# A one-column GELU on ScalarE behind its DMA issues, so that one table set serves an early copy and the GELUs

## The chip, the core and the metric

The kernel runs on one core of a Trainium2 chip. The metric is the device time of one execution, in microseconds (us). A kernel is run several times; medians and ranges are given. Engines are named as the profile names them: PE (matmul), PEld (PE's weight loads), ACT (ScalarE), DVE (VectorE), POOL (GpSimd), SP (its queue issues most DMAs). PSUM is the memory that PE writes its results to. A table load (`ACT_TABLE_LOAD` in the traces) is an instruction that the compiler puts on ACT; in before there is one ahead of the first copy, one ahead of the first GELU and one ahead of the first exp. A "slab" of a weight is 128 of its rows.

## The reference, cut to what matters

Two mixers read the same `x` (2048 x 512) and their results are blended with a gate. The change touches only the start of the second mixer, B:

```python
def _B_ref(x, w_in, w_sp, b_sp, w_out):
    Fh = w_in.shape[-1] // 2                      # 688
    z = gelu_tanh(x @ w_in)
    z1, z2 = z[..., :Fh], layernorm(z[..., Fh:])
    g = w_sp @ z2 + b_sp                          # over the sequence
    return (z1 * g) @ w_out
# mixer A: softmax feature maps (exp), linear attention; later in the kernel
# out = g * A(x) + (1 - g) * B(x)
```

## The kernel before: the parts that matter

The kernel first computes `z2` and `z1` tile by tile (128 rows each): PE multiplies, and ACT applies GELU to the result in PSUM and writes it to `z2all` or `z1all`. Later come the exps of mixer A. At the start, rows 0 to 255 of `x` arrive by plain DMA in `xs` and are transposed on PE; three of the four transposed pieces are copied to `xT` by DVE, and one by ACT:

```python
nc.sync.dma_start(out=xs[:, 0, :], in_=x2[0:P, :])
nc.scalar.dma_start(out=w_z2[:, 0, 0:HF], in_=w_in_v[:, 0, FH:FH + HF])
nc.sync.dma_start(out=xs[:, 1, :], in_=x2[P:2 * P, :])
load_z2w(nc.scalar, 1)            # w_z2 slabs 1..3 on ACT's DMA queue
load_z2w(nc.scalar, 2)
nc.sync.dma_start(out=w_z2[:, 0, HF:FH], in_=w_in_v[:, 0, FH + HF:F])
load_z2w(nc.scalar, 3)
x_dma_T(2, 2)                     # rows 256..511 of x, transposing DMA
for h in range(2):                # w_z1
    nc.sync.dma_start(out=w_z1[:, 2 * h:2 * h + 2, :], in_=...)
for i in range(4, 8):
    x_dma_T(i)
# ...
def zp_tile():                    # three PSUM tiles in turn
    return psA.tile([P, 2, CH], FP32, name="zp", tag=next_turn("zp", 3))

def z2_out(tt, zp):
    nc.scalar.activation(out=z2v, in_=zp[:, :, 0:HF], func=AF.Gelu_apprx_tanh)
    nc.vector.tensor_copy(out=glog[:, tt:tt + 1], in_=zp[:, 1, HF:HF + 1])
    # ... bn_stats, bn_aggr on DVE

def z2_first_two():               # tiles 0 and 1; order of PE's work
    warm_up(6); warm_up(2, P)     # matmuls on constants
    x_T(0, 0, 1, ...); x_T(0, 1, NDT, ...)
    warm_up(3, P)
    one(0, 0, 0)                  # one(tile, slab of w_z2, half)
    x_T(1, 0, 2, ...)
    x_T(1, 2, NDT, ..., on_act=True)     # <- the one copy on ACT
    one(0, 1, 0); warm_up(1, P); one(1, 0, 0); one(1, 1, 0)
    gate_T()
    one(0, 2, 0); one(1, 2, 0)
    for dt in range(1, 3):
        one(0, dt, 1); one(1, dt, 1)
    for tt in range(2):
        one(tt, 3, 0); one(tt, 0, 1); one(tt, 3, 1)
        z2_out(tt, zps[tt])       # <- the first GELU
# then z2_tile(2), z2_tile(3), z1 tiles 0..3, z2 tiles 4..7, ...
# b_T() (a small matmul on "brow") stands behind z1 tile 7

def x_T(i, d0, d1, tp, on_act=False):
    # ... PE transposes into tp
    if on_act:
        nc.scalar.copy(out=dst, in_=tp)
    else:
        nc.vector.tensor_copy(out=dst, in_=tp)
```

The softmax here doesn't subtract the row's maximum and nothing guards it: scores larger than these inputs give would overflow.

Of the kernel before, what the change touches and what calls it, by code (L numbers as in the profile page):

```python
# [7 lines left out]
AF = mybir.ActivationFunctionType  # L8
# [3 lines left out]
BF16 = mybir.dt.bfloat16  # L12
I32 = mybir.dt.int32

P = 128
# [20 lines left out]
def kernel(  # L36
# [14 lines left out]
    nc = tc.nc  # L51
# [6 lines left out]
    early = early_cm.__enter__()  # L58
# [45 lines left out]
        out=ramp[:, 0, :], data0=ones32[:, :], data1=zeros[:, :], initial=0.0,  # L104
# [4 lines left out]
    for q in range(4):  # L109
        qs = slice(32 * q, 32 * q + 32)  # L110
        nc.vector.tensor_tensor(
            out=ident[qs, qs], in0=ramp[qs, 0, :], in1=ramp[qs, 1, :], op=ALU.is_equal)
# [3 lines left out]
    def load_z2w(eng, dt):  # L116
        eng.dma_start(out=w_z2[:, dt, 0:FH], in_=w_in_v[:, dt, FH:F])  # L117
# [5 lines left out]
    load_z2w(nc.scalar, 2)  # L123
    nc.sync.dma_start(out=w_z2[:, 0, HF:FH], in_=w_in_v[:, 0, FH + HF:F])
    load_z2w(nc.scalar, 3)

    def x_dma_T(i, n=1):
        nc.sync.dma_start_transpose(out=xT[:, :, i * P:(i + n) * P], in_=x2[i * P:(i + n) * P, :])

    x_dma_T(2, 2)  # L130
    for h in range(2):
        nc.sync.dma_start(
            out=w_z1[:, 2 * h:2 * h + 2, :], in_=w_in_v[:, 2 * h:2 * h + 2, 0:FH])
    for i in range(4, 8):
        x_dma_T(i)
    for q in range(2, NCH):
        nc.sync.dma_start_transpose(
            out=xT[:, :, q * CH:(q + 1) * CH], in_=x2[q * CH:(q + 1) * CH, :]
        )
    nc.sync.dma_start(out=brow[0:NT, :], in_=B_b_sp.rearrange("(t p) -> t p", p=P))  # L140
    for qk in (1, 0):
        nc.sync.dma_start_transpose(
            out=wqkT[:, qk * NDT:(qk + 1) * NDT, :], in_=A_wqkv[:, qk * D:(qk + 1) * D])
# [4 lines left out]
    for h in range(2):  # L148
        nc.sync.dma_start(
            out=wv_sb[:, 2 * h:2 * h + 2, :],  # L150
            in_=A_wqkv[h * 2 * P:(h + 1) * 2 * P, 2 * D:3 * D].rearrange("(dt p) n -> p dt n", p=P),
        )
    for q in range(NCH):
        nc.sync.dma_start_transpose(
            out=wspT[:, :, q * CH:(q + 1) * CH], in_=B_w_sp[q * CH:(q + 1) * CH, :]
# [4 lines left out]
        out=mask4[:], in_=mask4[:], pattern=[[-32, NG]],  # L160
# [3 lines left out]
        out=mask4[:], in_=mask4[:], pattern=[[32, NG]],  # L164
# [3 lines left out]
        out=mask64[:, :, :], in_=mask4[:, :, None].to_broadcast([P, NG, DH]))  # L168
# [428 lines left out]
```

## Time and profile before

| what | before |
|---|---|
| time, median of 3 | 207.93 us (207.68 to 208.12) |
| span of the profiled execution | 206.3 us |
| PE busy | 202.2 us (98%) |
| ACT busy | 76.5 us (37%) |
| table loads on ACT | 3, of 1.28 us each |

These are lines of the page of before: busy time of each engine, with its share of the span and the number of instructions, then the chain that ended last by engine.

```profile
PE 202.2 (98%) x1536; PEld 120.3 (58%) x1536; DVE 128.8 (62%) x276; ACT 76.5 (37%) x123; POOL 45.4 (22%) x73
...
PE 95%; DMA 2%; ACT 1%; ACTq 0%; DVE 0%; issue 0%
```

PE is busy nearly throughout and is 95% of the chain. A change on ACT can only pay where PE waits for ACT. The view of waits for PE from 6.4 us on (engine, line, what was waited for: total us, times, longest) has just one line, and it names a DMA:

```profile
PE zp L188 <- DMA w_z<-in_B_w_in_dram: 0.2, 1, 0.2
```

The timeline of ACT at the start (start in us, duration in us, engine, line, operation; in brackets the idle time before it and what ended it) shows where its tables are loaded:

```profile
1.25 1.44 ACTq L117 DMA_DIRECT2D w_z<-in_B_w_in_dram  x3
2.72 1.28 ACT L275 ACT_TABLE_LOAD   x1 [2.72 <-issue]
5.28 0.37 ACT L275 COPY xT<-pq 128x256 bf16<-128x256 bf16 x1 [1.27 <-PE pq L272]
5.67 1.28 ACT L203 ACT_TABLE_LOAD   x1
7.92 1.38 ACT L203 ACTIVATE z2all<-zp 128x688 bf16<-128x688 f32 x2 [0.97 <-PE zp L188]
```

The load at 2.72 us belongs to the copy, the one at 5.67 us to the first GELU. After this second load ends at 6.95 us, ACT still waits 0.97 us for PE. The chain of waits in order of time says what PE waited for: the DMA of `w_z2`.

```profile
1.74 4.62 DMA w_z<-in_B_w_in_dram
...
6.41 15.65 PE zp L188 x106
```

### The profile page before, as it was taken

What the parts mean: (1) busy time and instruction counts of PE and PEld (TensorE: products, weight loads), DVE (VectorE), ACT (ScalarE), POOL (GpSimd) and SP (SyncE); (2) the same over time, 40 slices, a digit from 0 to 9 for tenths busy, and PEclk for the clock granted to TensorE, in tenths of its full rate; (3) what the DMA queues carried; (4) which work ended last, traced back from release to release, by engine and by line L of the source; (5) the groups of instructions that cost most, each with busy time, mean ns of one, the idle gap of its engine ahead of it and who ended that gap; (6) DMA issues with size and microseconds to landing.
All of it is one profiled execution on the core that took longest, in us unless ns stands there. A gap on an engine that the chain in (4) does not pass through costs nothing.

```text
span 206.3 us, 3946 instructions
## 1 busy us (share of the span) xinstructions
PE 202.2 (98%) x1536; PEld 120.3 (58%) x1536; DVE 128.8 (62%) x276; ACT 76.5 (37%) x123; POOL 45.4 (22%) x73
## 2 busy tenths in 40 slices
PE   8999999999999999999999999999999999999994
PEld 4566666655666555556565666555455555665642
DVE  3367565746977777979797778555466553633330
ACT  2756677796222243333424032222251126001322
POOL 5020202020522326244242422222204220200000
PEclk9999999999999999999999999999999999999999
DMA  6999499999998025940443229763554767353642
GB/s 169 268 199 182 91 235 210 253 210 248 208 290 147 3 38 131 322 93 15 88 28 64 51 38 117 144 115 73 105 153 89 79 104 190 58 104 70 129 91 78
DMA packets 90099, 27.22 MB, mean 132 GB/s; under 512 B 84224, under 2 KB 90080, under 8 KB 90080
## 3 DMA queue, kind: packets, MB, share of 16 engines
q1 hardware_dynamic: 87168, 24.28, 62.0%
q10 hardware_dynamic: 2880, 2.68, 4.1%
q8 instruction: 12, 0.20, 0.4%
q14 instruction: 7, 0.06, 0.1%
q0 software_dynamic: 32, 0.00, 0.0%
HBM read 4.15 MB, written 2.10 MB: 30 GB/s over the span
## 4 chain that ended last, share of the span: by engine, by line
PE 95%; DMA 2%; ACT 1%; ACTq 0%; DVE 0%; issue 0%
PE mm L441 36%; PE zp L188 17%; PE mm L346 14%; PE mm L480 8%; PE mm L478 7%; PE mm L386 7%; DMA w_z<-in_B_w_in_dram 2%; PE at L454 2%; PE kvacc L402 2%; PE mm L483 1%; PE zp L299 0%; ACT z1all L252 0%; ACT wq_p L306 0%; ACTq L117 0%; ACTq L120 0%; PE pq L299 0%
## 5 line engine op out<-in xcount | busy, mean ns | idle before, releaser
L441 PE MATMUL mm<-z2all,wspT 128*128 128x344 bf16 x512 | 79.9, 309 | 0.0
L441 PEld LDWEIGHTS <-wspT 128*128 128x128 bf16 x512 | 49.0, 98 | 25.7 <-issue 0.4
L188 PE MATMUL zp<-w_z,xT 128*128 128x344 bf16 (+1 forms) x256 | 38.9, 312 | 0.2 <-DMA w_z<-in_B_w_in_dram 0.2
L350 ACT ACTIVATE eq<-mm 128x512 bf16<-128x512 f32 x32 | 17.4, 594 | 51.3 <-PE mm L346 21.3
L354 DVE TENSOR_REDUCE zs<-eq 128x64 f32<-128x1024 bf16 x16 | 19.5, 1220 | 20.3 <-ACT eq L350 20.3
L188 PEld LDWEIGHTS <-xT 128*128 128x128 bf16 x256 | 24.9, 98 | 12.4 <-issue 0.3
L446 DVE SCALAR_TENSOR_TENSOR ucat<-mm,bT,z1all 128x344 bf16<-128x344 f32 x32 | 17.4, 544 | 21.9 <-PE mm L441 21.9
L363 POOL TENSOR_TENSOR eq<-eq,ratio 128x512 bf16<-128x512 bf16 x16 | 16.9, 1059 | 49.9 <-DVE ratio L362 41.7
L350 ACT ACTIVATE ek<-mm 128x512 bf16<-128x512 f32 x32 | 17.3, 600 | 27.4 <-PE mm L346 27.4
L494 ACT ACTIVATE ob<-mm,g_inv 128x512 bf16<-128x512 f32 (+1 forms) x16 | 10.9, 681 | 32.8 <-PE mm L483 28.3
L354 DVE TENSOR_REDUCE zs<-ek 128x64 f32<-128x1024 bf16 x16 | 19.3, 1210 | 2.8 <-ACT ek L350 2.8
L480 PE MATMUL mm<-wspT,uT 128*128 128x512 bf16 (+2 forms) x85 | 20.1, 366 | 0.0
L346 PEld LDWEIGHTS <-xT 128*128 128x128 bf16 x128 | 12.2, 98 | 13.2 <-PE mm L483 0.8
L363 POOL TENSOR_TENSOR ek<-ek,ratio 128x512 bf16<-128x512 bf16 x16 | 17.0, 1059 | 2.1 <-DVE ratio L362 1.5
L478 PE MATMUL mm<-wspT,oT 128*128 128x512 bf16 (+2 forms) x68 | 16.6, 366 | 0.0
L346 PE MATMUL mm<-wq_p,xT 128*128 128x512 bf16 x64 | 16.4, 379 | 0.0
L386 PE MATMUL mm<-wv_sb,xT 128*128 128x512 bf16 x64 | 16.4, 379 | 0.0
L346 PE MATMUL mm<-wk_p,xT 128*128 128x512 bf16 x64 | 16.3, 379 | 0.1
L206 DVE BATCH_NORM_STATS2 bn<-z2all 128x6 f32<-128x344 bf16 x32 | 14.9, 503 | 0.0
L203 ACT ACTIVATE z2all<-zp 128x688 bf16<-128x688 f32 x16 | 11.8, 744 | 6.3 <-PE zp L188 6.3
L252 ACT ACTIVATE z1all<-zp 128x688 bf16<-128x688 f32 x16 | 11.9, 744 | 5.1 <-PE zp L188 4.6
L480 PEld LDWEIGHTS <-uT 128*128 128x128 bf16 x85 | 8.1, 98 | 9.2
(72 smaller groups left out, 142.7 us busy)
## 6 DMA issues: line engine op xcount, KB each, us to landing
out_dram<-ob ACTq DMA_DIRECT2D x15, 128.0 KB, 1.7
wspT<-in_B_w_out_dram SPq DMA_DIRECT2D x2, 640.0 KB, 5.2
w_z<-in_B_w_in_dram SPq DMA_DIRECT2D x2, 344.0 KB, 5.2
w_z<-in_B_w_in_dram ACTq DMA_DIRECT2D x3, 172.0 KB, 4.6
wv_sb<-in_A_wqkv_dram SPq DMA_DIRECT2D x2, 256.0 KB, 3.5
wspT<-in_A_wo_dram SPq DMA_DIRECT2D x2, 256.0 KB, 3.9
xs<-in_A_x_dram SPq DMA_DIRECT2D x2, 128.0 KB, 2.7
uT<-ucat SPq DMA_TRANSPOSE x16, 2.8
```

The source lines that it names most:

```text
L188: nc.tensor.matmul(zp[:, j, 0:n], lhsT=xT[:, dt, tt * P:(tt + 1) * P], rhs=wt[:, dt, j * HF:j * HF + n], start=(dt == first), stop=(dt == ...
L206: nc.vector.bn_stats(out=bn6[:, tt, j, :], in_=z2v[:, j, :])
L252: nc.scalar.activation(out=z1all[:, tt, :].rearrange("p (j n) -> p j n", j=2), in_=zp[:, :, 0:HF], func=AF.Gelu_apprx_tanh,)
L346: nc.tensor.matmul(ps[:, :], lhsT=xT[:, dt, tt * P:(tt + 1) * P], rhs=w[:, dt, :], start=(dt == 0), stop=(dt == NDT - 1))
L350: nc.scalar.activation(out=e[:, :, a, :], in_=ps[:, :].rearrange("p (h f) -> p h f", f=DH), func=AF.Exp, scale=1.0 - 2.0 * a)
L354: nc.vector.tensor_reduce(out=z[:].rearrange("p h a -> p (h a)"), in_=e[:].rearrange("p h a f -> p (h a) f"), axis=AX.X, op=ALU.add,)
L363: nc.gpsimd.tensor_tensor(out=e[:, :, 1, :], in0=e[:, :, 1, :], in1=ratio[:, :, None].to_broadcast([P, H, DH]), op=ALU.mult)
L386: nc.tensor.matmul(v_ps[:, :], lhsT=xT[:, dt, tt * P:(tt + 1) * P], rhs=wv_sb[:, dt, :], start=(dt == 0), stop=(dt == NDT - 1))
L441: nc.tensor.matmul(gp[:, 0:HF], lhsT=wspT[:, st, tt * P:(tt + 1) * P], rhs=z2all[:, st, j * HF:(j + 1) * HF], start=(st == 0), stop=(st == ...
L446: nc.vector.scalar_tensor_tensor(out=ucat[tt % NU][:, c0 + j * HF:c0 + (j + 1) * HF], in0=gp[:, 0:HF], scalar=bT[:, tt:tt + 1], in1=z1all[ ...
L478: nc.tensor.matmul(acc, lhsT=oT[:, g, :], rhs=wo_t[:, g, c0:c1], start=(g == 0), stop=False)
L480: nc.tensor.matmul(acc, lhsT=uT[:, i + ft, :], rhs=w_main[i][:, ft, c0:c1], start=False, stop=False)
```

## The change

The intent: ACT needs GELU's table anyway, and the copy is taken to run under that table too. If a GELU stands ahead of the copy, the first load is GELU's own and the second goes. The new GELU works on one column of a constant and its result is not used.

```diff
--- before.py
+++ after.py
@@ -123,6 +123,9 @@
     load_z2w(nc.scalar, 2)
     nc.sync.dma_start(out=w_z2[:, 0, HF:FH], in_=w_in_v[:, 0, FH + HF:F])
     load_z2w(nc.scalar, 3)
+    scrap = early.tile([P, 1], BF16, name="scrap")
+    nc.scalar.activation(
+        out=scrap[:, :], in_=nc.const_aps.tensor(1.0, [P, 1], BF16), func=AF.Gelu_apprx_tanh)
 
     def x_dma_T(i, n=1):
         nc.sync.dma_start_transpose(out=xT[:, :, i * P:(i + n) * P], in_=x2[i * P:(i + n) * P, :])
```

## The prediction

> What bounds the kernel now. The page gives PE 202.2 us busy of a 206.3 us span (98%), and the chain that ended last is 95% PE, 1% ACT. The waits view of PE from 6.41 us on lists one wait, 0.2 us on the DMA of w_z2, and none on ACT. The chain over the first 30 us runs: DMA issues on ACT's queue (to 1.72 us), the DMA of w_z2 (1.74 to 6.36 us), then PE from 6.41 us without a break (zp x124 in 18.27 us, 147 ns each).
>
> What the change removes. The timeline of ACT has three table loads of 1.28 us: at 2.72 us (for the copy to xT), at 5.67 us right after that copy (for the first GELU), and at 45.58 us (for the first exp). With a one-column GELU behind ACT's last DMA issue, the first load is GELU's own, and the copy needs no other: the Trainium skill, "ScalarE: Activation LUTs", section "Table sets: the hidden batching unit", says that cheap functions such as copy appear in every set. The compiled order agrees: one load before the one-column GELU, none between copy and first GELU. So the load at 5.67 to 6.95 us goes. The section "What ACT_TABLE_LOAD costs" gives 1283 ns for the load, as this trace does, and about 1380 ns for a drain; the trace shows no extra drain before the second load, which starts 0.02 us after the copy.
>
> What it adds. One ACTIVATE of 128x1, which I estimate at 0.2 us from the 744 ns of 128x688 and the 594 ns of 128x512. It runs at about 4.0 us, and waits only for a constant that POOL has written by 0.5 us. ACT idles 1.27 us before the copy at 5.28 us (waiting for PE's transposes), so it costs nothing. The tile adds 2 bytes a partition; the order of instructions on PE, DVE, POOL and SP is unchanged.
>
> How much is on the critical path: nothing. After the second load ACT still waits 0.97 us for PE before the first GELU at 7.92 us. That GELU cannot start sooner: its last matmul is the ninth since 6.41 us (6.41 + 9 x 0.147 = 7.73, plus some 0.2 us to the result), and those nine wait for the w_z2 DMA, whose issues lie ahead of the change. ACT only becomes idle longer. Even a later GELU would not stall PE at once: PE next needs its bank at about 9.3 us (an estimate: 7.73 + 11 x 0.147), and it is free at about 8.9 us.
>
> Predicted time: 207.9 us, as before (207.68 to 208.12), range 207.4 to 208.3. Faster by over 2%: 0.01; within 2%: 0.98; slower by over 2%: 0.01.
>
> What would show each step. Right: ACT has two table loads and about 1.1 us less busy time (76.5 to 75.4); the first stays at 2.7 us and the copy to xT at 5.28 us; ACT's idle time before the first GELU grows from 0.97 to about 2.25 us, still ended by PE; that GELU starts at 7.92 us within 0.1 us; the span stays within 0.3 us of 206.3. Wrong: the first GELU starts early, or PE's unbroken run starts before 6.3 us.
>
> What would make it wrong. The copy might run otherwise under the GELU set, or the one-column GELU might hold ACT past 5.24 us; either would show as a later copy and a PE wait on ACT. The w_z2 DMA might land at another time from run to run, which moves everything by a few tenths of a us without the change having a part in it.

## The result, and the profile after

| | before | after |
|---|---|---|
| time, median of 4 runs each | 208.00 us (207.68 to 208.12) | 207.81 us (207.64 to 208.03) |
| span of the profiled execution | 206.3 us | 206.3 us |
| ACT busy | 76.5 us | 75.4 us |
| table loads on ACT | 3 | 2 |
| copy to xT on ACT starts at | 5.28 us | 4.64 us |
| first GELU starts at | 7.92 us | 8.00 us |

The ratio is 0.9994, with a 95% interval of 0.9976 to 1.0011: the same. A ratio here is the mean time of one kernel's fast runs over that of the other's fast runs of the same rounds, so it is not quite the ratio of the medians quoted.

The same lines of the page of after. PE's 200.5 us are the sum over 1518 recorded matmuls instead of 1536 (a trace can miss some); they are no gain.

```profile
PE 200.5 (97%) x1518; PEld 119.5 (58%) x1536; DVE 128.8 (62%) x276; ACT 75.4 (37%) x123; POOL 45.4 (22%) x73
...
PE 94%; DMA 2%; ACT 1%; issue 1%; ACTq 0%; DVE 0%
```

The timeline of ACT after the change:

```profile
2.72 1.28 ACT L127 ACT_TABLE_LOAD   x1 [2.72 <-issue]
4.02 0.21 ACT L127 ACTIVATE scrap<-const-bfloat16-1.0 128x1 bf16<-128x1 bf16 x1
4.64 0.37 ACT L278 COPY xT<-pq 128x256 bf16<-128x256 bf16 x1 [0.42 <-PE pq L275]
8.00 1.38 ACT L206 ACTIVATE z2all<-zp 128x688 bf16<-128x688 f32 x2 [2.98 <-PE zp L191]
```

The load at 5.67 us is gone, and the one-column GELU costs 0.21 us at 4.02 us. Nothing follows from it: the first GELU starts at 8.00 us, still released by PE, and ACT has only waited longer (2.98 us instead of 0.97). The wait of PE that lies in the chain is again for the same DMA, which landed 0.08 us later in this execution, and the GELU is 0.08 us later with it:

```profile
1.75 4.70 DMA w_z<-in_B_w_in_dram
...
6.49 15.64 PE zp L191 x106
```

Before that, PE waits 0.5 us for the DMA of the gate's row in this execution (0.3 us in before_again, not at all in before); PE had come that far sooner than in before, and gained nothing by it.

One thing was not foreseen: the copy moved by 0.64 us, although nothing that it depends on was changed. The first experiments ask whether the change did that.

A useful mark came out of comparing the traces. From the small matmul on `brow` (at about 24.5 us) to PE's last matmul, 178.68 us pass in both kernels (24.52 to 203.20 and 24.59 to 203.27). So the length of these executions is settled in the first 24 us, and the start of the brow matmul can be used to compare starts more finely than the total time does.

### The profile page after: what moved, and what is told of

Same layout as the page of the kernel before. It is cut to its first block, busy times and chain, and to the rows that moved or that the text cites. A ratio compares the mean times of both kernels' runs of the same rounds, so it can differ in the third digit from the quotient of the medians.

```text
span 206.3 us, 3933 instructions
## 1 busy us (share of the span) xinstructions
PE 200.5 (97%) x1518; PEld 119.5 (58%) x1536; DVE 128.8 (62%) x276; ACT 75.4 (37%) x123; POOL 45.4 (22%) x73
## 4 chain that ended last, share of the span: by engine, by line
PE 94%; DMA 2%; ACT 1%; issue 1%; ACTq 0%; DVE 0%
PE mm L444 36%; PE zp L191 17%; PE mm L349 13%; PE mm L483 8%; PE mm L389 7%; PE mm L481 7%; DMA w_z<-in_B_w_in_dram 2%; PE at L457 2%; PE kvacc L405 2%; PE mm L486 1%; PE zp L302 0%; ACT z1all L255 0%; ACT wq_p L309 0%; ACTq L117 0%; ACTq L120 0%
## 5 line engine op out<-in xcount | busy, mean ns | idle before, releaser
L191 PE MATMUL zp<-w_z,xT 128*128 128x344 bf16 (+1 forms) x256 | 38.4, 309 | 0.5 <-DMA w_z<-in_B_w_in_dram 0.4
L481 PE MATMUL mm<-wspT,oT 128*128 128x512 bf16 (+2 forms) x62 | 15.6, 365 | 0.3
```

Source lines behind the costliest of these rows:

```text
L191: nc.tensor.matmul(zp[:, j, 0:n], lhsT=xT[:, dt, tt * P:(tt + 1) * P], rhs=wt[:, dt, j * HF:j * HF + n], start=(dt == first), stop=(dt == ...
L481: nc.tensor.matmul(acc, lhsT=oT[:, g, :], rhs=wo_t[:, g, c0:c1], start=(g == 0), stop=False)
```

## The experiments

Theory 1: the removed load lay in slack. The first GELU waits for PE, and PE's start is set by DMAs and by PE's own pace; ACT comes after both. Rivals: (2) the change has a small gain, hidden in noise or given back by the added ACTIVATE; (3) a table switch costs more than the 1.28 us that the load shows, so that the true gain was bigger and was lost elsewhere; (4) table loads never bound this kernel at all, wherever they stand. In the tables below "first GELU" and "brow" are starts of instructions in the profiled execution.

| run | median us (range) | ratio to before, 95% | copy on ACT | first GELU | brow |
|---|---|---|---|---|---|
| before_again | 207.85 (207.70 to 208.18) | 0.9998 (0.9985 to 1.0011) | 5.24 | 8.12 | 24.72 |
| after_again | 207.82 (207.75 to 208.36) | 0.9998 (0.9985 to 1.0012) | 5.28 | 7.85 | 24.45 |
| copy_dve | 207.94 (207.90 to 208.20) | 1.0012 (1.0000 to 1.0024) | none | 7.85 | 24.44 |
| load2 | 207.86 (207.79 to 208.28) | 1.0000 (0.9988 to 1.0013) | 5.28 | 8.48 | 24.84 |
| load3 | 211.65 (210.54 to 212.79) | 1.0192 (1.0147 to 1.0237) | 4.89 | 11.13 | 27.30 |
| load3_again | 212.55 (210.76 to 212.82) | 1.0206 (1.0174 to 1.0239) | 5.17 | 11.40 | 28.89 |
| load3_third | 212.81, one execution, state unknown | | 5.27 | 11.51 | 29.35 |
| load4 | 216.12 (215.32 to 216.40) | 1.0383 (1.0363 to 1.0404) | 4.70 | 13.96 | 32.91 |
| fast_before | 207.63 (207.29 to 208.17) | 0.9996 (0.9982 to 1.0010) | 5.28 | 7.24 | 24.15 |
| fast_after | 207.77 (207.65 to 208.30) | 1.0006 (0.9992 to 1.0019) | 5.14 | 7.21 | 24.23 |
| xT_later | 208.87 (208.38 to 208.97) | 1.0049 (1.0036 to 1.0062) | 4.99 | 8.49 | 25.13 |
| w1_later | 207.74 (207.20 to 208.12) | 0.9993 (0.9978 to 1.0008) | 5.27 | 7.59 | 24.18 |

In all fourteen profiles, brow to last matmul took 178.68 to 178.70 us. The kernel before, run beside them, had medians of 208.01 us (with before_again, after_again, load2 and load3), 207.79 us (with the two fast kernels, copy_dve and xT_later) and 207.89 us (with load3_again, load3_third, load4 and w1_later). All these kernels also gave the correct result by the comparison with the reference; for the two "fast" ones that only says that the comparison is too loose for an error in 256 rows of the branch.

### Both kernels again: noise, and the copy that moved

No edit; each kernel as it was.

> The kernel before, unchanged, as the measure of noise. Both theories: ratio 1.000 within 0.002. Theory 1 (the copy to xT moved from 5.28 to 4.64 us because PE came to full speed earlier in that one execution, not because of the change): in this profile the copy starts anywhere between 4.6 and 5.3 us, in step with the time at which PE's weight loads go from 0.15 to 0.10 us. Rival (the change itself moved the copy): it starts at 5.28 us again within 0.05 us. First GELU at 7.8 to 8.1 us, ended by PE.

> The changed kernel again, with more rounds. Theory (the removed load lay in slack of 0.97 us behind the w_z2 DMA and PE): ratio 1.000 within 0.002, two table loads, first GELU at 7.8 to 8.1 us, ended by PE. Rival (a small gain, of up to 0.6 us, is hidden by noise): ratio below 0.999 with its interval below 1. The copy to xT starts between 4.6 and 5.3 us; the rival for the copy wants 4.64 us again.

Both are at 0.9998 of before. The lower ends of the intervals (0.9985) leave room for a gain of 0.15% (0.3 us) at most. The copy to `xT` starts at 5.24 us in before and at 5.28 us in the changed kernel:

```profile
5.24 0.37 ACT L275 COPY xT<-pq 128x256 bf16<-128x256 bf16 x1 [1.24 <-PE pq L272]
5.28 0.37 ACT L278 COPY xT<-pq 128x256 bf16<-128x256 bf16 x1 [1.06 <-PE pq L275]
```

The first of these alone would not decide, as both theories allowed 5.24 us. The second does: the rival wanted 4.64 us again in the changed kernel. So the change alone does not move the copy. What differs is PE's pace. These are PE's weight loads around the transposes, first of the changed kernel's first profile (copy at 4.64 us), then of its second (copy at 5.28 us):

```profile
3.36 0.15 PEld L222 LDWEIGHTS <-const-bfloat16-1.0 128*128 128x128 bf16 x1 [0.28 <-issue]
3.47 0.27 PEld L275 LDWEIGHTS <-xs 128*128 128x128 bf16 x4
...
4.39 0.10 PEld L191 LDWEIGHTS <-xT 128*128 128x128 bf16 x1
```

```profile
3.36 0.15 PEld L222 LDWEIGHTS <-const-bfloat16-1.0 128*128 128x128 bf16 x1 [0.28 <-issue]
3.47 0.47 PEld L275 LDWEIGHTS <-xs 128*128 128x128 bf16 x4
...
4.93 0.15 PEld L191 LDWEIGHTS <-xT 128*128 128x128 bf16 x1
```

Four weight loads take 0.27 us in one execution and 0.47 in the other, and a single one 0.10 against 0.15. PE starts slowly in every execution and comes to full pace at a moment that differs. The packed traces also hold records of the granted clock, which the views above don't print. The first record, at full clock, begins at 3.46 us in the first profile and at 6.64 us in the second, and from there on the weight loads take 0.10 us in both, where most of those before took 0.15. In the thirteen profiles that have such a record (xT_later has none), it begins between 3.46 and 6.64 us. The Trainium skill, "TensorE: Matmul & The Clock Gate", section "Part 1: The HAM clock gate (the "warmup" mystery)", explains such a moment: PE runs at half clock until it has been busy for a window of 3413 ns, and the window is free-running, so the moment depends on where in a window the kernel starts. The traces agree: all their clock records are whole multiples of 3413 ns long (59 of them in before, 60 in after), except the last ones, which are cut off by the end of the profile. That PE's business in such a window is what decides is the page's statement; the stalls of load3 and load4 below point the same way.

after_again also corrects the picture of the start: PE never waits for the `w_z2` DMA there. It gets through its slow start so late (its unbroken run of zp matmuls begins at 6.07 us, at first still at the slow pace) that the weights are already there, and the first GELU comes at 7.85 us all the same. Its view of waits for PE, over the whole span, has one line, the wait at the very start:

```profile
PE zp L222 <- PEq L584: 0.8, 1, 0.8
```

The DMA and PE's slow start are nearly tied, and which one ends last differs between executions. ACT is ready before both.

### The load removed without adding anything

```diff
-        x_T(1, 2, NDT, pq_tile([P, 2, P], BF16)[:, :, :], on_act=True)
+        x_T(1, 2, NDT, pq_tile([P, 2, P], BF16)[:, :, :])
```

> The kernel before with its one early ACT copy moved to DVE. The second load goes too, but with no added ACTIVATE: ACT has two table loads, the first one already GELU's at 2.7 us. Theory: the removed load is worth nothing on its own, so ratio 1.000 within 0.002. Rival (the added ACTIVATE gave back a real gain): ratio below 0.999. DVE takes some 0.3 us more before 5.7 us, in slack before the 6.2 us cast.

With its early copy on DVE, ACT's first instruction is a GELU, and there are two table loads without a dummy ACTIVATE. The timeline of ACT:

```profile
2.71 1.28 ACT L203 ACT_TABLE_LOAD   x1 [2.71 <-issue]
7.85 1.38 ACT L203 ACTIVATE z2all<-zp 128x688 bf16<-128x688 f32 x2 [3.85 <-PE zp L188]
```

ACT now waits 3.85 us for PE, and the ratio is 1.0012 (1.0000 to 1.0024): not below 0.999. The copy is now work for DVE, but the view of PE's waits names no DVE. So the added ACTIVATE did not eat a gain. Rival 2 falls, but for a gain too small for these times (0.3 us, above), and the traces, in which the first GELU waits for PE in every run without extra loads, give no reason for one.

### More loads: how large is the slack, and what does a switch cost

The changed kernel with one-column ACTIVATEs behind the copy, whose functions alternate between the two table sets:

```diff
             nc.scalar.copy(out=dst, in_=tp)
+            nc.scalar.activation(out=scrap[:, :], in_=<ones, one column>, func=AF.Exp)                # load2
+            nc.scalar.activation(out=scrap[:, :], in_=<ones, one column>, func=AF.Gelu_apprx_tanh)    # load3: and these two
+            nc.scalar.activation(out=scrap[:, :], in_=<ones, one column>, func=AF.Exp)
+            # load4: one more GELU, exp pair
```

Between the copy and the first GELU this puts two loads (load2), four (load3) and six (load4); before has one, the changed kernel none.

> The changed kernel with a one-column exp behind the copy to xT: two table loads between that copy and the first GELU (before has one, the changed kernel none). Theory (a switch costs ACT the 1.28 us of the load alone, and there is about 0.97 us of slack on ACT and some 0.4 us more in PE's banks): ACT is ready 2.8 us after the copy ends, at 7.8 to 8.5 us; the first GELU is 0 to 0.6 us late; time within 0.4 us of before. Rival (each switch costs a further drain of about 1.38 us): ACT is ready at 10.5 to 11.2 us and the time rises by about 2 us.

The timeline of ACT in load2:

```profile
5.28 0.37 ACT L278 COPY xT<-pq 128x256 bf16<-128x256 bf16 x1 [1.05 <-PE pq L275]
5.66 1.28 ACT L279 ACT_TABLE_LOAD   x1
6.96 0.21 ACT L279 ACTIVATE scrap<-const-bfloat16-1.0 128x1 bf16<-128x1 bf16 x1
7.18 1.28 ACT L206 ACT_TABLE_LOAD   x1
8.48 2.13 ACT L206 ACTIVATE z2all<-zp 128x688 bf16<-128x688 f32 x3
```

From the end of the copy (5.65 us) to the first GELU pass 2.83 us: two loads of 1.28, one ACTIVATE of 0.21, and 0.06 us of gaps. The GELU no longer waits for PE. In before it comes 1.51 us after PE's unbroken run starts (6.41 to 7.92); here that run starts at 6.74 us, so it would have come at 8.25 us and is 0.23 us late. PE doesn't notice: its view of waits lists no ACT and no DVE, and the time is that of before. So the first GELU may even be late by a little, as predicted from the three PSUM tiles (PE needs the first tile's PSUM again only for its fourth tile). The Trainium skill, "ScalarE: Activation LUTs", section "What ACT_TABLE_LOAD costs", adds a drain of about 1380 ns to the load of 1283 ns. The load agrees (1283 ns in the groups of instructions here); the drain doesn't show in these traces, and two of them would have put the GELU at about 11.2 us. Rival 3 falls.

> The same with one-column exp, GELU and exp behind the copy: four table loads between the copy and the first GELU. Theory: ACT is ready 5.9 us after the copy ends, at 10.9 to 11.5 us; the first GELU is about 3 us late, PE stalls at the fourth tile for 2.4 to 3.1 us, and the time rises to about 210.5 us (210.0 to 211.2). Rival with the drain: ready at 16.3 to 16.9 us, time about 216 us. Rival 2 (table loads never bound this kernel): time unchanged.

In load3 the first GELU starts at 11.13 us. Its view of waits for PE:

```profile
PE zp L191 <- DVE glog L207: 2.2, 1, 2.2
...
PE zp L191 <- DMA w_z<-in_B_w_in_dram: 0.3, 1, 0.3
```

The stall in the timeline of PE:

```profile
12.12 4.10 PE L191 MATMUL zp<-w_z,xT 128*128 128x344 bf16 x27 [2.24 <-DVE glog L207]
```

The 0.3 us are the wait for `w_z2`, as in before. New is that PE waits 2.24 us for the `glog` copy on DVE, which waits for the GELU, and the chain that ended last now runs through all four loads. Reckoned as above, the GELU is 2.83 us late (PE's run starts at 6.79 us, so 8.30 us would have been its time), and PE loses 2.24 of it: the three PSUM tiles absorb 0.59 us. So a table load on the critical path does cost time here, and rival 4 falls. The profiled execution took 210.77 us, as expected (210.5 us); the stall is a little shorter than expected (2.24 us, not 2.4 to 3.1). But the four times fell into two pairs, 210.5 and 210.8, then 212.5 and 212.8 us, and the median is above my range. That needed an explanation.

### Why four loads cost either about 2.7 or about 4.7 us

> The kernel with four table loads before the first GELU, again, because its four times fell in two pairs: 210.5 and 210.8, 212.5 and 212.8 us. Its profile (210.77 us) shows PE idle for 2.24 us from 9.9 us and at full pace afterwards. Theory A: in the slower executions PE falls back to its slow pace after that idle time (weight loads of 0.15 us instead of 0.10 for some us), which adds about 2 us; the times again fall near 210.6 and 212.7, and a profile of a slow one shows such weight loads after 12 us and a span near 211 us. Theory B: the spread comes from the landing of DMAs; then a slow profile shows PE waits on DMA instead.

> A third profile of the same kernel, to catch the other of its two times. Same expectations: near 210.6 us with weight loads of 0.10 us after the stall, or near 212.7 us with some us of 0.15 us weight loads (Theory A), or PE waits on DMA (Theory B).

> Six table loads between the copy and the first GELU. ACT is ready 6 x 1.30 + 5 x 0.22 = 8.9 us after the copy ends, at 13.9 to 14.6 us; PE stalls at the fourth tile until about 15 us, for 5 to 5.6 us. Theory A (PE falls back to its slow pace after long idle time): every execution does so, with weight loads of 0.15 us after 15 us, and the time rises by the stall and about 2 us more, to 214.8 to 216 us, with no second group of times 2 us apart. Theory B: only the stall counts: 213 to 213.8 us.

Over the nine executions of load3, three took 210.5 to 210.8 us and six 212.3 to 212.8 us. The first profile is of the faster group, the other two are of the slower one. Here are stretches of 2 us (bounds in us, length, PE's busy time with the number of matmuls, granted PE clock, DMA share, GB/s), first of load3, then of load3_third:

```profile
12.00:14.00 2.00, 1.88 (x13) 1.00 1.20 197
14.00:16.00 2.00, 2.00 (x16) 1.00 1.09 202
16.00:18.00 2.00, 2.00 (x16) 1.00 0.76 169
```

```profile
12.00:14.00 2.00, 1.50 (x6) 0.66 1.15 243
14.00:16.00 2.00, 2.00 (x8) 0.50 1.19 226
16.00:18.00 2.00, 2.00 (x16) 0.99 0.82 142
```

The stall ahead of it in load3_third:

```profile
12.50 3.74 PE L191 MATMUL zp<-w_z,xT 128*128 128x344 bf16 x13 [3.33 <-DVE glog L207]
```

After the stall PE does 16 matmuls in a stretch in load3, but 8 in load3_third, where the granted clock is 0.50, and the weight loads take 0.15 us again until it ends. Nothing there waits for a DMA. In stretches of 0.2 us the clock is at 0.50 from about 11.7 to 15.1 us in load3_again and from about 12.6 to 16.0 us in load3_third, 3.4 us each time. In load4, whose stall is 6.19 us (5 to 5.6 were expected), it is at 0.50 from about 13.8 to 20.6 us, and all four executions are slow, at 215.3 to 216.4 us (a little above what I expected), without a second group 2 us apart. In load3 the idle time was 2.24 us and the clock stayed up.

So theory A holds: after these longer stalls PE falls back to half clock, and it works on at half pace until the phase ends. In load3_third PE works at half clock from 12.62 to 16.04 us by the clock records, which costs half of that, 1.71 us, on top of the stall of 3.33 us. The sum can be checked at the brow mark: load3_third is 2.05 us behind load3, and PE was released 0.38 us later in it (12.50 us against 12.12), which with 1.71 gives 2.09. The same sum gives 1.63 for load3_again (measured 1.59) and 5.68 for load4 (measured 5.61). (The stall itself is longer there than in load3 because PE, in that execution, had begun its run at 5.93 us instead of 6.79, and ACT was ready 0.38 us later.) The page on TensorE named above has both the half clock and the window of 3413 ns, in the same section; these slow phases of 3.4 us, and of twice that in load4, agree with it: by the clock records they last 3413 ns and twice that. How long a stall must be is not separated from where it lies: the stall of load3 is not only shorter but lies across two windows (7.73 to 11.15 and 11.15 to 14.56 us, counted in steps of 3413 ns from its first clock record at 4.32 us), with over 2 us of work in each. It is also why an ACT delay cannot be reckoned by its length alone.

### Taking the DMA wait away

The first two tiles read only slabs of `w_z2` that land early (slab 0's first half, slab 1), and the gate column is made after them. Their outputs are wrong, which doesn't matter for the times.

```diff
-            z_one(zps[tt], tt, w_z2, FH + 1, dt, j, first=j)
+            n, c0 = HF + j, j * (HF - 1)
+            nc.tensor.matmul(
+                zps[tt][:, j, 0:n], lhsT=xT[:, dt, tt * P:(tt + 1) * P],
+                rhs=w_z2[:, j if dt == 0 else 1, c0:c0 + n],
+                start=(dt == j), stop=(dt == NDT - 1))
...
-        gate_T()
         one(0, 2, 0)
...
             z2_out(tt, zps[tt])
+        gate_T()
```

> The kernel before, with the first two z2 tiles reading only the w_z2 slabs that land early, and the gate column made after them. Results are wrong on purpose (about 12% of the z2 rows); it takes the wait on the last w_z2 DMA off the first GELU. Theory (that DMA, not ACT, sets the start): PE begins the tiles' matmuls at about 5.4 to 5.6 us instead of 6.4, the first GELU starts at 6.9 to 7.2 us, in before now close to the end of the second table load (6.3 to 6.95 us), and the time falls by 0.5 to 0.9 us, unless the next DMA (w_z2's last slabs or the third tile's xT) is then waited for at about 7.2 us. Rival (ACT and its table loads set the start): the time stays.

> The same edit on the changed kernel. Theory: even with the DMA wait gone, the load of before ends before PE has the first tile, so this equals fast_before within 0.2 us, with the first GELU at the same time within 0.15 us. Rival (the removed load is worth its 1.28 us once the DMA is out of the way): 0.5 us or more faster than fast_before.

The first GELUs, from the timelines of ACT, first fast_before, then fast_after:

```profile
5.67 1.28 ACT L203 ACT_TABLE_LOAD   x1
7.24 1.38 ACT L203 ACTIVATE z2all<-zp 128x688 bf16<-128x688 f32 x2 [0.29 <-PE zp L226]
```

```profile
5.14 0.37 ACT L284 COPY xT<-pq 128x256 bf16<-128x256 bf16 x1 [0.92 <-PE pq L281]
7.21 1.38 ACT L206 ACTIVATE z2all<-zp 128x688 bf16<-128x688 f32 x2 [1.70 <-PE zp L229]
```

With the DMA out of the way the first GELU comes 0.7 us sooner (7.24 us against 7.92), and the second load of before, which ends at 6.95 us, is still ahead of it, by 0.29 us. Both kernels have the GELU within 0.03 us of each other, and their ratios (0.9996 and 1.0006) don't differ. So even with the earliest start that I could give PE, the load costs nothing. The hoped-for gain did not come: the time did not fall by 0.5 to 0.9 us, and the expectation's own proviso, another wait close behind, held instead. The brow matmul comes only 0.37 and 0.29 us sooner than in the first profile of before, and the total times don't show even that. Part of the head start is given back at the third tile: in fast_before the chain runs through the cast of the gate column on DVE at 7.72 us (which my edit had moved there), and in fast_after PE waits for the third tile's `xT`, which lands at 7.82 us. The next DMA stood close behind the one removed.

### Moving the DMAs, in search of a faster kernel

Nothing in these two edits concerns tables; they ask whether the start can be had sooner.

```diff
# xT_later
-    x_dma_T(2, 2)
     for h in range(2):
         nc.sync.dma_start(out=w_z1[:, 2 * h:2 * h + 2, :], in_=...)
+        if h == 0:
+            x_dma_T(2, 2)

# w1_later
     x_dma_T(2, 2)
+    x_dma_T(4)
     for h in range(2):
         nc.sync.dma_start(out=w_z1[:, 2 * h:2 * h + 2, :], in_=...)
-    for i in range(4, 8):
+    for i in range(5, 8):
         x_dma_T(i)
```

> The kernel before with the first transposing load of x (rows 256 to 511) issued behind the first half of w_z1, to leave the DMA engines to w_z2. Theory (the w_z2 DMA sets PE's start at 6.4 us): if w_z2 lands earlier, PE starts earlier by as much, at most 0.6 us, and the time falls by the same, unless the transposed load then arrives after about 8.2 us, where PE wants it; then the time stays or rises. I expect within 0.6 us of before either way. No use of the table loads in it.

> The kernel before with the w_z1 loads issued one transposing load later, to leave the DMA engines to w_z2; with rows 256 to 511 of x loaded behind w_z1 the w_z2 DMA landed at 7.82 us instead of 6.37, so w_z1 seems to be what holds it up. Theory: w_z2 lands up to 0.4 us earlier, PE's unbroken run starts up to 0.4 us earlier, and since from the brow matmul to the last matmul all kernels take 178.68 us, the time falls by as much: 207.5 to 207.9 us. If w_z1 then lands after about 10.5 us, where PE wants it, the time rises instead.

xT_later is slower, at 1.0049 (1.0036 to 1.0062), about 1 us and more than the 0.6 us that I had allowed. The chain of waits in it:

```profile
2.23 5.59 DMA w_z<-in_B_w_in_dram
...
7.86 4.15 PE zp L189 x27
```

The last slab of `w_z2` lands at 7.82 us, against 6.37 us for the slab that before waits for. With this edit the first half of `w_z1` is issued at 2.21 us instead of 3.83 us, beside the slabs of `w_z2` that PE needs first. That the two share the DMA engines would explain it; the run shows only that the landing is later. The profiled execution loses 0.61 us at the brow mark, less than the medians differ; the rest stays open.

w1_later does what was expected of it at the start: PE waits for no DMA, its run begins at 5.93 us, and the first GELU is at 7.59 us. The brow mark is 0.34 us sooner than in before's first profile. But the times, 207.20 to 208.12 us, are not separable from those of before (0.9993, interval 0.9978 to 1.0008). No kernel beats before by a margin that the runs show.

## Why the prediction was right

The prediction was 207.9 us in a range of 207.4 to 208.3 us; the measured median is 207.81 us. Point by point:

- **The load goes.** Right: two table loads instead of three, ACT's busy time from 76.5 to 75.4 us. The copy ran for the same 0.37 us under GELU's table. The Trainium skill, "ScalarE: Activation LUTs", section "Table sets: the hidden batching unit", on which this rested, agrees with the trace: no load stands between the one-column GELU and the copy, or between the copy and the first GELU.
- **The added ACTIVATE.** Estimated at 0.2 us, measured 0.21 us, in idle time of ACT.
- **Nothing of it on the critical path.** Right. The first GELU was at 8.00 us (7.92 within 0.1 us was predicted), released by PE. copy_dve shows that the load was worth nothing even without the dummy; fast_before and fast_after show that it would still be worth nothing if PE released the first GELU 0.7 us sooner; load2 shows that a delay of a few tenths at the GELU is absorbed; load3 shows that the same loads do cost time once the slack is used up. The slack was thus measured, not only read.
- **Slack behind the GELU.** Predicted from the PSUM tiles as the difference between 9.3 and 8.9 us, about 0.4 us; load3 gives 0.59 us.
- **The `w_z2` DMA ends the wait.** Right in the profiles of before and after, but too narrow. In after_again PE does not wait for it; PE's own slow start ended last there, and PE's unbroken run began at 6.07 us. A start before 6.3 us was one of the prediction's own signs of being wrong; it came with no gain and no early GELU (7.85 us), so the sign was a poor one and the forecast stood. The GELU's time is the later of the two.
- **The copy stays at 5.28 us.** Wrong in the profile of after (4.64 us), and with it the idle time before the first GELU (2.98 us instead of 2.25). The step that failed is the assumption that PE's transposes take the same time in every execution. after_again, with 5.28 us in the same changed kernel, shows that the change alone does not do it, and xT_later, built from before, has the copy at 4.99 us without it.

## What to carry to other kernels

In this kernel a table load cost nothing as long as ScalarE would have waited anyway. Before removing one, read in the timeline whether ScalarE's first real work after the load was released by the load or by another engine, and how long it waited. If it waited, removing the load only makes the wait longer. To measure such slack rather than argue it, add the suspected cost once, twice and more until the time moves; and expect the time to jump beyond the stall when PE stands idle for long: here the stalls of 3.33 us and more came with a phase of 3.4 us or more at half clock, that of 2.24 us did not.

## What the Trainium skill lacked or had wrong

- "ScalarE: Activation LUTs", section "What ACT_TABLE_LOAD costs": about 1380 ns of drain and 2.66 us in total for every switch. Here a switch took ACT 1.28 us and 0.01 to 0.02 us of gaps, in before (copy end to load: 0.02 us) and in load2 to load4, where loads and one-column ACTIVATEs follow one another every 1.52 us (5.66, 7.18 us).
- "TensorE: Matmul & The Clock Gate", the table of states in Part 1, lets the clock drop after at least one idle window of about 3.4 us. In load3_again the clock dropped at about 11.7 us, when PE had been idle for only about 2.7 us (since 9.0 us, where the profile models the end of its last matmul). The window that ended there, 8.29 to 11.71 us counted in steps of 3413 ns from that trace's clock records, so held some 0.7 us of work and counted as idle all the same. An idle time of 2.24 us, split between two windows (load3), was not enough.
- No page that I read says that a profile can lack clock records for the slow start: in before the first record begins at 5.90 us, in xT_later there is none, and the views print 1.00 where there is no record (over the first 2.7 us of before, for one), while PE's weight loads take 0.15 us instead of 0.10 until after 5 us. The end of the slow start and the later fall to 0.50 after a stall are in the records.
- No page that I read warns that PE's moment of full pace shifts instructions of other engines, too: the same ACT copy started between 4.64 and 5.28 us in executions of the same kernel.
